# Fused attention and MLP on one core: the copy of a finished half of the context bank moved behind all contexts of its phase

## The chip, the core and the metric

The kernel runs on one NeuronCore of a Trainium2 chip. The engines that matter here are TensorE (PE, with PEld for its weight loads), VectorE (DVE), ScalarE (ACT), GpSimd (POOL) and SyncE (SP); POOL and SP mostly issue DMAs. Each engine works through its own instructions in order, and engines wait for each other through semaphores. The metric is the time of one execution on the device in microseconds (us), taken as a median of runs.

## What is computed

Two branches are computed from the same input `x` (2048 rows of 512, float32), and a gate per row mixes them:

```python
g = sigmoid((x * gate_w).sum(-1, keepdims=True))
# A: attention, 32 query heads of 16, one shared key/value head
q = (x @ wq).reshape(1, 2048, 32, 16).transpose(0, 2, 1, 3)
k, v = x @ wk, x @ wv
p = softmax(einsum("bhqd,bkd->bhqk", q, k) * 16 ** -0.5)
a = einsum("bhqk,bkd->bhqd", p, v).transpose(0, 2, 1, 3).reshape(1, 2048, 512) @ wo
# B: MLP with squared ReLU, 512 -> 1792 -> 512
b = square(maximum(x @ w1 + b1, 0)) @ w2 + b2
out = g * a + (1 - g) * b
```

## The kernel before

**Attention.** The queries are cut into 4 column chunks of 512 positions and 8 groups of 4 heads, so there are 32 *iterations* `it`, and each has two halves `q` of 256 positions. For one half there are 16 key tiles of 128 keys. One *unit* `u` is one key tile of one half for the four heads: a score matmul pair (`score`, line 765) gives 128 keys x 4 heads x 256 positions, ACT takes the exponential into a tile `e` (`exps`, L802), and the *context* of the unit (`context`, L824) multiplies it with the values and adds it up in PSUM. There are 1024 units. Half of a score goes through a PSUM tile `s` of two banks, of which there are two; other scores go through a one-bank tile `x`, from which DVE copies them into `e` first (`score_copy`, L786), and ACT then works on `e` in place. The tile `e` is kept in five buffers of two units each.

**The context bank.** All contexts add up in one PSUM bank, the tile `acc` of 512 columns (`both`). The columns 0 to 255 (`accs[0]`) belong to the half `q = 0` of an iteration and the columns 256 to 511 (`accs[1]`) to `q = 1`. The four heads of a unit go to the four 32-partition quarters of the bank. When the 16th context of a half is done, `finish` copies the 256 columns to an SBUF tile `accs` (on ACT, L882; on DVE, L878 and L930, in the last two iterations). The dependency between the copy and the matmuls is kept for the tile, and not for its columns: a context that is written in program order behind the copy waits until the copy is done, also where it adds to the other half.

**Phases.** PE's instructions are written phase by phase. A `phase` takes some slots of a unit of the projections or the MLP (`M` in the table `PLANS`, L1141; two of them run on two halves of the rows) and puts score matmuls between them (`S0`, `S1`, ... through `s`; `02`, `13` and the like through `x`). Behind it comes `context(range(u, u + m))`, which issues the contexts of `m` units in one go, most often 7 or 6. The scores run ahead of the contexts by `AHEAD` = 4 units, so at the start of a run of contexts ACT still has the exponentials of the phase in its queue, which belong to the contexts of the phases behind. Sixteen is no multiple of 7 or 6, so a half mostly ends inside a run of contexts:

```python
for u in us:
    it, kt, q = place(u)
    ...
    if kt == NK - 1:
        finish(it, q)
```

**Behind the copy.** When both halves of an iteration are copied, SP moves the sums and the denominators to the tiles `oc` and `lq` (L889, L890). Every second iteration `divide` puts four pieces of work on a list for DVE: clamp and test the denominators (`n`, L857 and L858), take the reciprocal (L851), whereupon POOL writes it to DRAM (`ls`, L852) and spreads it with eight DMAs to the tile `lc` (L854), and multiply `oc` with `lc` (L861). Their places among DVE's other work follow from the planner's own clock (`at_pe`, `at_act`, `at_dve`), with fixed allowances: `DIVIDES` = 10 from the copy to the clamp, `SPREADS` = 8 from the reciprocal to the product. The planner's clock holds 0.41 for the copy on ACT and nothing for a wait of the contexts behind it.

Of the kernel before, what the change touches and what calls it, by code (L numbers as in the profile page):

```python
# [14 lines left out]
AF = mybir.ActivationFunctionType  # L15
# [40 lines left out]
HC = CH // 2  # L56
# [109 lines left out]
def mix_kernel(ctx: ExitStack, tc: tile.TileContext, xT, wkv, wq, wo, w12, b1, b2, cst, out):  # L166
    nc = tc.nc
# [63 lines left out]
    with fast, tc.tile_pool(name="at", bufs=1) as at, \  # L231
# [176 lines left out]
        def qnorm(tiles, p8=None):  # L408

            if p8 is None:  # L410
                p8 = aside()
            n = 32 * len(tiles)
            for i, (it, sq) in enumerate(tiles):
                nc.tensor.matmul(p8[32 * i:32 * i + 32], blk, sq, start=True, stop=True, tile_position=(0, 32 * i))
            nrm, tmp = of_tile("nrm"), of_tile("tmp", F32)
            root(nrm[:n], p8[:n], tmp[:n])
            if tiles[0][0] == 0:
                q_direct(RS, nrm, 1, (nc.sync, nc.gpsimd))
            for i, (it, sq) in enumerate(tiles):
                o = qs[it, 0, DH]  # L420
                nc.sync.dma_start(bass.AP(tensor=o.tensor, offset=o.offset,
                                          ap=[[KS * 2 * CH, 4], [CH, 2], [1, CH]]),
                                  nrm[32 * i:32 * i + 8].bitcast(F32))
                done.update((it, it + 1))
# [26 lines left out]
        def act(d, ready=0.0):  # L451

            nonlocal at_act
            at_act = max(at_act, ready) + d
            return at_act

        def dve(d, ready=0.0):

            nonlocal at_dve
            at_dve = max(at_dve, ready) + d  # L460
            return at_dve
# [284 lines left out]
        def place(u):  # L746

            it, k = divmod(u, 2 * NK)
            return (it, k % NK, k // NK) if it else (it, k // 2, k % 2)
# [56 lines left out]
        accs = [None, None]  # L806

        def context(us):

            nonlocal at_pe  # L810
            at_pe += 0.12
            for u in us:
                it, kt, q = place(u)
                at_pe = max(at_pe, made[u] + 0.06) + CONTEXT
                if not both:
                    both.append(ap.tile([128, CH], F32, name="acc"))
                n = 1
                if it == 0:
                    if q == 0:
                        continue  # L820
                    q, n, u = 0, 2, u - 1
                accs[q] = both[0][:, q * HC:q * HC + HC * n]
                for h in range(4):
                    nc.tensor.matmul(accs[q][h * 32:(h + 1) * 32], v_ext[:, kt],  # L824
                                     es[u // 2][:, h % 2 * 2 + h // 2, u % 2 * HC:u % 2 * HC + HC * n],
                                     start=(kt == 0), stop=(kt == NK - 1),
                                     skip_group_check=True, tile_position=(0, h * 32))
                if it == 0:
                    accs[:] = both[0][:, :HC], both[0][:, HC:]
                    if kt == NK - 1:  # L830
                        finish(0, 0)
                    q = 1
                if kt == NK - 1:
                    finish(it, q)
            if narrow:
                at_pe = max(at_pe + 0.2, used_x[0] + 0.05)
                qnorm(narrow.pop(0))
                late.append(True)
                used_x[0] = dve(1.3, at_pe + 0.2) + 0.06
            at_pe += 0.24  # L840
# [21 lines left out]

        sums = []

        def finish(it, q):

            c, gr = divmod(it, NG)
            t, u = divmod(gr, 2)
            if it == NC * NG - 1:
                if q == 0:  # L870
                    side.append(half(accs[0], 0))
                    next(side[-1])
                return
            if q == 0:
                sums.append(at.tile([128, CH], F32, name="accs"))
            a = sums[-1]
            if it == NC * NG - 2:
                nc.vector.tensor_copy(a[:, q * HC:q * HC + HC], accs[q])  # L878
                if q:
                    side.append(turn(a, 0, range(4), LAST_OK))  # L880
                return
            nc.scalar.activation(a[:, q * HC:q * HC + HC], accs[q], AF.Copy)  # L882
            act(0.41, at_pe)
            if q == 0:
                return
            if u == 0:
                ol[c, t] = at.tile([128, CH], F32, name="oc", bufs=2), at.tile([128, LW], F32, name="lq", bufs=2)
            o, l = ol[c, t]
            nc.sync.dma_start(o[u * 64:u * 64 + 64], a[0:128:2])  # L889
            nc.sync.dma_start(l[u * 64:u * 64 + 64], a[1:128:32].rearrange("h (b n) -> h b n", n=LW))  # L890
            if u == 1:
                divisions.extend(divide(o, l, 4 * c + t, at_act + (LANDS if (c, t) == (NC - 1, 2) else DIVIDES)))

                def done():
                    nc.gpsimd.dma_start(oTs[it - 1:it + 1].rearrange("u d n -> (u d) n"), o)
                    complete.add((c, t))

                divisions.append((0.0, 0.0, done))
# [3 lines left out]
        def turn(a, u, js, okc, idle=0):  # L902

            if not o2:
                o2.append(at.tile([128, 4, 2, 4, DH], F32, name="o2", tag="oc", bufs=2))
            js = slice(js[0], js[-1] + 1)
            m = js.stop - js.start
            if m > 2:
                yield
            tp = aside().rearrange("p (j n) -> p j n", j=4)  # L910
            for j in range(m):
                nc.tensor.transpose(tp[:, j], a[:, j * 128:(j + 1) * 128], ident)
            busy(idle)
            p5 = tp[:, :m].rearrange("p j (h d e) -> p j h d e", h=4, e=2)
            l = p5[:, :, :, 0, 1]
            n = at.tile([128, 2, 4, 4], F32, name="nl")[:, :, :m]
            nc.vector.tensor_scalar(n[:, 0], l, L_MIN, L_MAX, op0=OP.max, op1=OP.min)
            nc.vector.scalar_tensor_tensor(n[:, 1], n[:, 0], 1.0, l, op0=OP.mult, op1=OP.is_equal,
                                           accum_out=ok[:, okc:okc + 1])
            nc.vector.reciprocal(n[:, 0], n[:, 0])  # L920
            nc.vector.tensor_tensor(o2[0][:, js, u], p5[:, :, :, :, 0],
                                    n[:, 0].unsqueeze(3).to_broadcast([128, m, 4, DH]), OP.mult)
# [3 lines left out]
        def half(acc, q):  # L926

            js = range(2 * q, 2 * q + 2)
            a = at.tile([128, CH], F32, name="ah", tag="accs" if q else "lc", bufs=1 if q else 2)
            nc.vector.tensor_copy(a[:, :HC], acc)  # L930
            busy(2 * q)
            if not q:
                yield
                yield
            yield from turn(a, 1, js, LAST_OK + 1 + q, 3 * q)
            if q:
                okm = at.tile([128, 1], F32, name="okm")
                nc.vector.tensor_reduce(okm, ok[:, :LAST_OK + 3], AX.X, OP.add)
            else:
                yield  # L940
            r, w = of_tile("or"), of_tile("ol")
            tq = mp.tile([128, CH], F32, name="mm")
            for j in js:
                nc.tensor.transpose(tq[:, j % 2 * 128:j % 2 * 128 + 128],
                                    o2[0][:, j].rearrange("p u h d -> p (u h d)"), ident)
            if q:

                pf = mp.tile([1, 1], F32, name="mm")
                nc.tensor.matmul(pf, okm, cs[:, C_ONE:C_ONE + 1], start=True, stop=True)
                busy(3)  # L950
            nc.scalar.activation(r[:, :HC], tq[:, :HC], AF.Copy)
            if q:
                nc.vector.tensor_scalar(bad, pf, 128.0 * LW * NC * KT - 0.5, None, op0=OP.is_lt)
            nc.vector.tensor_tensor(w[:, :HC], tq[:, :HC], r[:, :HC].bitcast(F32), OP.subtract)
            last[q] = r, w
# [3 lines left out]
        def busy(n):  # L959

            if n and not junk:
                junk.append(sp.tile([128, 2, CH], F32, name="s")[:, 0])
            for _ in range(n):
                nc.tensor.matmul(junk[0], cs[:, :64].bitcast(BF), cs[:, :CH // 2].bitcast(BF), start=True, stop=True)
# [146 lines left out]
        side, units, ended = [], work(), []  # L1111
# [163 lines left out]
        while u < total:  # L1275
# [8 lines left out]
            it = (u + m - 1) // (2 * NK)  # L1284
# [57 lines left out]
```

## Time and profile before

| what | value |
|---|---|
| median of 3 runs | 1387.97 us (1386.97 to 1388.77) |
| profiled execution | 1385.57 us |
| its span, first to last instruction | 1383.8 us |
| PE busy | 1246.4 us (90%) |
| ACT busy | 1060.9 us (77%) |
| DVE busy | 742.4 us (54%) |
| mean granted TensorE clock | 0.957 |
| copies of a half on ACT (L882) | 60, of 385 ns |

The span is the time from the first to the last instruction of the profiled execution; the execution's own time is 1.8 us longer. A share of busy time says how long an engine held an instruction, not how well it was used: the end of a matmul is modelled, and the granted clock tells how fast the array ran. A matmul of the kernel's float32 contexts stands twice in the profile (7 units of 4 heads are 56 rows), since each is run as two passes.

### The profile page before, as it was taken

To read this page: it belongs to the slowest core of one execution; us is meant where nothing else is said; L and a number is where in the kernel's file an instruction comes from. 1 tells how busy PE (TensorE), PEld (TensorE's weight loads), DVE (VectorE), ACT (ScalarE), POOL (GpSimd) and SP (SyncE) were. 2 spreads that over 40 slices of the span, in tenths; PEclk is the share of its full clock that TensorE was granted. 3 is DMA by queue.
4 is the path that set the end of the run, shared out by engine and by line. 5 is a ranking of instruction groups with operands and counts; after the bars stand their busy time and mean duration, and the time that the engine had idled before them with its cause. 6 is when DMAs were issued, how large, how long until landed. Compare 5 with 4: busy or idle time off the path is not lost.

```text
span 1383.8 us, 31763 instructions
## 1 busy us (share of the span) xinstructions
PE 1246.4 (90%) x13686; PEld 801.9 (58%) x13686; DVE 742.4 (54%) x1221; ACT 1060.9 (77%) x1211; POOL 132.4 (10%) x222
## 2 busy tenths in 40 slices
PE   9998889989889899889888988998898889889997
PEld 4565556656556566556555655665565556555663
DVE  6765474656535754537535644646436745547333
ACT  6787686878677887779786877887877868778873
POOL 1002011010010201101012010100102102010100
PEclk9999899999999999999998999999999999999999
DMA  6244321111222212101222212101112212110100
GB/s 218 72 110 108 86 81 43 37 60 52 66 70 70 78 55 86 62 17 50 82 62 79 70 47 86 56 24 48 59 58 78 78 40 94 35 39 30 35 37 33
DMA packets 49338, 89.71 MB, mean 65 GB/s; under 512 B 14362, under 2 KB 14858, under 8 KB 48680
## 3 DMA queue, kind: packets, MB, share of 16 engines
q1 hardware_dynamic: 36664, 64.58, 15.0%
q0 software_dynamic: 12384, 22.77, 5.4%
q8 instruction: 109, 1.79, 0.6%
q14 instruction: 37, 0.30, 0.1%
q10 hardware_dynamic: 144, 0.26, 0.1%
HBM read 61.76 MB, written 21.22 MB: 60 GB/s over the span
## 4 chain that ended last, share of the span: by engine, by line
PE 46%; issue 34%; ACT 11%; POOL 4%; DMA 3%; DVE 2%; DVEq 0%; POOLq 0%; ACTq 0%
PE acc L824 19%; PE mm L1141 14%; PE s L765 9%; ACT e L802 9%; PE x L765 2%; POOL lc L854 2%; DMA ls<-n 1%; DMA lc<-ls 1%; POOL res L697 1%; ACT accs L882 1%; DVE e L786 1%; ACT w2r L500 1%; POOL qs L358 1%; DVE oc L861 0%; ACT w1r L500 0%
## 5 line engine op out<-in xcount | busy, mean ns | idle before, releaser
L802 ACT ACTIVATE e<-s 128x1024 f32<-128x1024 f32 x762 | 749.2, 1027 | 288.1 <-PE s L765 234.6
L786 DVE COPY e<-x 128x512 f32<-128x512 f32 x524 | 362.4, 692 | 573.5 <-PE x L765 461.9
L824 PE MATMUL acc<-e,v_ext 128*32 128x256 f32 (+1 forms) x8064 | 528.3, 410 | 120.9 <-ACT accs L882 119.3
L824 PEld LDWEIGHTS acc<-e,v_ext 128*32 128x32 f32 x8064 | 252.9, 115 | 357.7 <-ACT accs L882 144.3
L765 PE MATMUL s<-qa,k_aug 49*128 49x512 f32 x1524 | 444.8, 418 | 0.1
L765 PEld LDWEIGHTS s<-qa,k_aug 49*128 49x128 f32 x1524 | 235.8, 187 | 98.2 <-ACT e L802 48.6
L802 ACT ACTIVATE e<-e 128x1024 f32<-128x1024 f32 x262 | 277.1, 1058 | 5.8 <-DVE e L786 5.7
L765 PE MATMUL x<-qa,k_aug 49*128 49x512 f32 x524 | 221.7, 423 | 6.3 <-DVE e L786 4.0
L1141 PE MATMUL mm<-w2r,hr 64*128 64x512 f32 x752 | 159.7, 396 | 0.0
L765 PEld LDWEIGHTS x<-qa,k_aug 49*128 49x128 f32 x524 | 97.9, 187 | 35.2 <-DVE e L786 10.6
L1141 PEld LDWEIGHTS mm<-w2r,hr 64*128 64x128 f32 x752 | 108.4, 190 | 13.6 <-issue 0.8
L1141 PE MATMUL mm<-w2l,hr 64*128 64x512 f32 x376 | 92.4, 392 | 0.0
L852 POOL DMA_DIRECT2D ls<-n x15 | 8.5, 564 | 689.4 <-DVE n L851 616.8
L1141 PE MATMUL mm<-xragain,w1r 64*128 64x512 f32 x224 | 67.6, 398 | 0.0
L1141 PE MATMUL mm<-xlagain,w1r 64*128 64x512 f32 x224 | 67.0, 394 | 0.0
L1141 PE MATMUL mm<-xr,w1r 64*128 64x512 f32 x224 | 66.0, 397 | 0.0
L1141 PE MATMUL mm<-xl,w1r 64*128 64x512 f32 x224 | 65.8, 394 | 0.0
L1141 PEld LDWEIGHTS mm<-w2l,hr 64*128 64x128 f32 x376 | 58.4, 186 | 6.6
L854 POOL DMA_DIRECT2D lc<-ls x120 | 58.3, 494 | 30.9 <-DMA ls<-n 30.7
L1141 PE MATMUL mm<-more 64*128 64x512 f32 x216 | 58.5, 394 | 0.0
L1141 PE MATMUL mm<-xragain,w1l 64*128 64x512 f32 x224 | 51.3, 392 | 0.0
L1141 PE MATMUL mm<-xr,w1l 64*128 64x512 f32 x224 | 50.5, 392 | 0.0
(169 smaller groups left out, 1223.3 us busy)
## 6 DMA issues: line engine op xcount, KB each, us to landing
stage<-in_w SPq DMA_DIRECT2D x56, 256.0 KB
qa<-qs SPq DMA_DIRECT2D x186, 64.0 KB
w1f<-in_w SPq DMA_DIRECT2D x28, 256.0 KB
w2f<-in_w SPq DMA_DIRECT2D x28, 256.0 KB
qs<-qr SPq DMA_DIRECT2D x16, 256.0 KB
ress<-res POOLq DMA_DIRECT2D x4, 1024.0 KB, 4.5
qs<-ql POOLq DMA_DIRECT2D x15, 256.0 KB, 7.9
oc<-accs SPq DMA_DIRECT2D x30, 128.0 KB
```

What stands on the lines that cost most here:

```text
L358: eng.dma_start(bass.AP(tensor=o.tensor, offset=o.offset, ap=[[KS * 2 * CH, 4], [CH, 2 * DH], [1, CH]]), src.bitcast(F32))
L500: nc.scalar.activation(out, src, AF.Copy)
L697: nc.gpsimd.tensor_scalar(part, b2t[0], omg[:, s:s + 1], None, op0=OP.mult)
L765: nc.tensor.matmul(dst.rearrange("p (a n) -> p a n", a=2), k_aug[rows, kt * 128:(kt + 1) * 128], qa[it][rows, :, q * HC:q * HC + HC], star ...
L786: nc.vector.tensor_copy(e_half(u)[:, 2 * r:2 * r + 2], x.rearrange("p (a n) -> p a n", a=2))
L802: nc.scalar.activation(e_half(u), src, AF.Exp, scale=SCALE)
L824: nc.tensor.matmul(accs[q][h * 32:(h + 1) * 32], v_ext[:, kt], es[u // 2][:, h % 2 * 2 + h // 2, u % 2 * HC:u % 2 * HC + HC * n], start=(k ...
L852: nc.gpsimd.dma_start(ls[i].rearrange("a (b n) -> (a b) n", b=16), n)
L854: nc.gpsimd.dma_start(wide[16 * k:16 * k + 16], bass.AP(tensor=ls.tensor, offset=ls[i, k].offset, ap=[[0, 16], [1, CH]]))
L882: nc.scalar.activation(a[:, q * HC:q * HC + HC], accs[q], AF.Copy)
L1141: nc.tensor.matmul((self.before if r else self).bank, a[p], b[p], start=not r and i == 0, stop=r == 1 and i == len(self.terms[1]) - 1, ski ...
```

## The change

Inside `context`, a finished half is no longer handed to `finish` at once. The function collects it, with the slice of the bank that it is in, and calls `finish` for all that were collected after the last context of the run has been written. `finish` takes the slice as an argument, because `accs` may have moved on to the next half by then.

```diff
             nonlocal at_pe
             at_pe += 0.12
+            ends = []
             for u in us:
...
                 if it == 0:
                     accs[:] = both[0][:, :HC], both[0][:, HC:]
                     if kt == NK - 1:
-                        finish(0, 0)
+                        ends.append((0, 0, accs[0]))
                     q = 1
                 if kt == NK - 1:
-                    finish(it, q)
+                    ends.append((it, q, accs[q]))
+            for end in ends:
+                finish(*end)
...
-        def finish(it, q):
+        def finish(it, q, acc):
...
-            nc.scalar.activation(a[:, q * HC:q * HC + HC], accs[q], AF.Copy)
+            nc.scalar.activation(a[:, q * HC:q * HC + HC], acc, AF.Copy)
             act(0.41, at_pe)
```

Where a half ends with the last context of a run, nothing moves. The order of the instructions on ACT, POOL and SP is the same as before in the whole program, and so is PE's; on DVE one clamp of denominators (L857), late in the program, stands behind two copies of scores in place of one. What changes is which instruction waits.

The first place is a run of seven contexts on PE, the one that the profile has at 202 us. `s`, `x` and `mm` are PSUM tiles of the scores and of the projections, `acc` is the context bank; a unit is four matmuls here. Before:

```order
L765 MATMUL s<-qa,k_aug 128x512 [waits Activation_49]
L1141 MATMUL mm<-xr_81,w1l 128x512
L765 MATMUL x<-qa,k_aug 128x512 [waits DVE_49]
L765 MATMUL s<-qa,k_aug 128x512
L824 MATMUL acc<-e,v_ext 32x256 x4
L824 MATMUL acc<-e,v_ext 32x256 [waits Activation_49]
L824 MATMUL acc<-e,v_ext 32x256 x23
L765 MATMUL s<-qa,k_aug 128x512 [waits PE_49]
```

The same place with the change:

```order
L765 MATMUL s<-qa,k_aug 128x512 [waits Activation_49]
L1144 MATMUL mm<-xr_81,w1l 128x512
L765 MATMUL x<-qa,k_aug 128x512 [waits DVE_49]
L765 MATMUL s<-qa,k_aug 128x512
L825 MATMUL acc<-e,v_ext 32x256 x28
L765 MATMUL s<-qa,k_aug 128x512 [waits Activation_49]
```

The second unit's first matmul had to wait for ACT, and 24 matmuls stood behind it; now the 28 matmuls have no wait among them. The first score of the next phase now names ACT itself; it needs the exponential that frees its tile `s`, which the wait inside the contexts had covered before.

The second place is ACT's queue at the same time: two exponentials, the rounding of a weight tile (`more`), the copy, and the first exponential of the next phase. Before:

```order
L802 ACTIVATE e<-e 128x4x256 [waits DVE_49]
L802 ACTIVATE e<-s 128x4x256
L500 ACTIVATE more<-stage 128x512
L882 ACTIVATE accs<-acc 128x256
L802 ACTIVATE e<-s 128x4x256 [waits PE_49,Activation_49]
```

With the change:

```order
L802 ACTIVATE e<-e 128x4x256 [waits DVE_49]
L802 ACTIVATE e<-s 128x4x256
L500 ACTIVATE more<-stage 128x512
L885 ACTIVATE accs<-acc 128x256 [waits PE_49]
L802 ACTIVATE e<-s 128x4x256 [waits PE_49,Activation_49]
```

The copy keeps its place in ACT's queue and now waits for PE there, for the contexts of the run that are written ahead of it.

More of the change, by code (lines that the diff above doesn't have):

```diff
@@ L870, in finish @@
                 if q == 0:
-                    side.append(half(accs[0], 0))
+                    side.append(half(acc, 0))
                     next(side[-1])
@@ L877, in finish @@
             if it == NC * NG - 2:
-                nc.vector.tensor_copy(a[:, q * HC:q * HC + HC], accs[q])
+                nc.vector.tensor_copy(a[:, q * HC:q * HC + HC], acc)
                 if q:
```

## The prediction

> **What bounds the kernel now.** The page's first part, busy time by engine, says that PE is nearest to its limit:
>
> ```profile
> PE 1246.4 (90%) x13686; PEld 801.9 (58%) x13686; DVE 742.4 (54%) x1221; ACT 1060.9 (77%) x1211; POOL 132.4 (10%) x222
> ```
>
> The waits by engine then say what stops PE, and what the others wait for (columns: total us, times, longest):
>
> ```profile
> PEld acc L824 <- ACT accs L882: 144.3, 52, 7.0
> PE acc L824 <- ACT accs L882: 119.3, 52, 6.6
> ...
> ACT e L802 <- PE s L765: 234.6, 134, 6.5
> ...
> PEld s L765 <- ACT e L802: 48.6, 123, 0.8
> ...
> DVE oc L861 <- DMA lc<-ls: 13.1, 9, 4.1
> ```
>
> One wait stands out: 52 of the 60 copies stop the context matmuls. The PE row counts from the modelled end of the last matmul and the PEld row from the last weight load, so the true stop lies between 119.3 and 144.3 us. ACT and DVE mostly wait for PE; neither is the pacer over the whole kernel.
>
> To see what one such stop is, I cut the stretch around 200 us at the phases' starts: a phase without a copy, the next phase's scores, the stop, the contexts left, and the phase after (columns: us, busy us of PE, PEld, DVE, ACT and POOL with counts, granted clock, DMA):
>
> ```profile
> 189.76:197.54 7.78, 7.78 (x99) 5.30 (x96) 6.81 (x12) 7.78 (x10) 0.00 (x0) 1.00 0.34 103
> 197.54:202.17 4.63, 4.63 (x43) 3.55 (x39) 2.85 (x5) 4.05 (x5) 0.00 (x0) 1.00 0.32 93
> 202.17:206.66 4.49, 0.64 (x10) 0.15 (x9) 3.16 (x5) 3.67 (x5) 0.00 (x0) 1.00 0.18 52
> 206.66:211.07 4.41, 4.41 (x48) 2.03 (x48) 0.00 (x0) 0.00 (x0) 0.00 (x0) 0.61 0.09 32
> ```
>
> The timelines of PE and of ACT show the cause:
>
> ```profile
> 202.17 0.64 PE L824 MATMUL acc<-e,v_ext 128*32 128x256 f32 x8
> 206.66 4.48 PE L824 MATMUL acc<-e,v_ext 128*32 128x256 f32 x48 [3.85 <-ACT accs L882]
> ```
>
> ```profile
> 204.80 1.01 ACT L802 ACTIVATE e<-s 128x1024 f32<-128x1024 f32 x1
> 205.71 0.63 ACT L500 ACTIVATE more<-stage 128x512 fp32r<-128x512 f32 x1
> 206.22 0.38 ACT L882 ACTIVATE accs<-acc 128x256 f32<-128x256 f32 x1
> 211.91 2.89 ACT L802 ACTIVATE e<-s 128x1024 f32<-128x1024 f32 x3 [5.30 <-PE s L765]
> ```
>
> The first context of the run closes a half. Its copy takes 0.38 us, but stands on ACT behind exponentials that are only needed by a later phase; PE idles 3.85 us for it with 48 matmuls queued. Two things follow. ACT, done at 206.6, idles 5.30 us, because the next scores come late: the time is lost to both. And the 48 matmuls run at a clock of 0.61 and take 4.41 us. Scores and contexts together took 13.53 us (197.54 to 211.07), where the phase ahead took 7.78 for as much work: 5.75 us lost by one copy.
>
> **What the change removes.** (a) *The stop.* The run of contexts has no wait in it any more. In the example 5.75 us are lost; 3.85 are the PE row's wait, and the clock costs (1 - 0.61) x 4.41 = 1.72, so 0.18 is missing from the PE row. With 0.2 on each of 52 waits, the stop is worth 119.3 + 10.4 = 130 us (bounds 119.3 and 144.3).
>
> (b) *The slow clock behind it.* The row of cores gives the clock over the span:
>
> ```profile
> core 0: 1383.8 us, clock 0.957
> ```
>
> That is (1 - 0.957) x 1383.8 = 59.5 us of lost full-clock time. Some of it passed while PE was idle anyway, as behind the longest stop (two windows, then windows behind two other stops, with those stops' rows of the timeline):
>
> ```profile
> 136.00:138.00 2.00, 0.00 (x0) 0.00 (x0) 1.42 (x3) 0.10 (x1) 0.83 (x2) 0.50 0.27 17
> 138.00:140.00 2.00, 0.00 (x0) 0.00 (x0) 1.76 (x3) 2.00 (x3) 0.16 (x1) 0.50 0.15 43
> ```
>
> ```profile
> 290.56:292.86 2.30, 2.30 (x40) 1.20 (x41) 0.00 (x0) 0.00 (x0) 0.00 (x0) 1.00 0.18 61
> ...
> 371.50:374.50 3.00, 3.00 (x24) 1.49 (x18) 0.00 (x0) 0.13 (x1) 0.00 (x0) 0.50 0.18 52
> ```
>
> ```profile
> 290.56 2.37 PE L824 MATMUL acc<-e,v_ext 128*32 128x256 f32 x40 [2.61 <-ACT accs L882]
> ```
>
> ```profile
> 371.03 2.58 PE L824 MATMUL acc<-e,v_ext 128*32 128x256 f32 x24 [2.08 <-ACT accs L882]
> ```
>
> Four idle us at 0.50 are 2 of the 59.5; with a few shorter ones and the span's ends I take 52 as paid by matmuls (bounds 40 and 59.5). [...]
>
> A check on (a) and (b) together: the contexts behind the first iteration are 7936 rows, 8 to a unit, so 992 units. A clean phase of seven takes 7.79 us; the first such phase starts at 70.35 and the last context ends at 1369.24.
>
> ```profile
> L824 PE MATMUL acc<-e,v_ext 128*32 128x256 f32 x7936 | 513.3, 407 | 120.9 <-ACT accs L882 119.3 <-DVE accs L878 1.1 <-DVE ah L930 0.5
> ```
>
> ```profile
> 646.05:653.84 7.79, 7.79 (x98) 5.23 (x94) 5.84 (x10) 6.39 (x8) 0.00 (x0) 1.00 0.11 34
> ```
>
> ```profile
> 70.35 0.49 PE L765 MATMUL s<-qa,k_aug 49*128 49x512 f32 x1
> ```
>
> ```profile
> 1368.60 0.64 PE L824 MATMUL acc<-e,v_ext 128*32 128x256 f32 x8
> ```
>
> 992 x 7.79 / 7 = 1104 us at the clean rate, 1298.9 in fact: 195 us are lost to everything. (a) and (b) claim 182 of them; the other 13 stay.
>
> **What it adds.** (c) *The copy waits for the rest of the run, and the next phase's exponentials queue behind it on ACT.* Eight copies already stand behind all contexts, because a half ended with its run. Two such phases, and the phase behind the second:
>
> ```profile
> 265.99:273.93 7.94, 7.94 (x98) 5.14 (x95) 5.80 (x10) 7.94 (x11) 0.00 (x0) 1.00 0.10 35
> 872.04:880.00 7.96, 7.96 (x99) 5.16 (x95) 5.85 (x10) 7.96 (x11) 0.00 (x0) 1.00 0.30 96
> 880.00:887.79 7.79, 7.79 (x100) 5.55 (x96) 6.47 (x14) 6.55 (x8) 2.52 (x5) 1.00 0.15 52
> ```
>
> They take 0.15 and 0.17 us more than 7.79; ACT is busy throughout, and in the next phase it has slack again (6.55 of 7.79). So 52 copies at 0.16 cost 8 us. Below, a copy could cost nothing where ACT has slack; above, its whole 0.38, which is 20 us. SP's move of the sums and POOL's spreading follow the copy as before; both only wait longer for it, in program terms by what was left of the run, and the loads queued behind SP's move go to tiles that DVE frees later.
>
> (d) *DVE's wait for the spread denominators.* From the reciprocal (L851) to the product (L861), the DMAs out and back take some 8.7 us, whatever PE does. Two cases on DVE, the first with no stop of PE between, the second with one, and that stop:
>
> ```profile
> 632.40 0.35 DVE L851 RECIPROCAL n<-n 128x32 f32<-128x32 f32 x1
> ...
> 641.11 0.69 DVE L861 TENSOR_TENSOR oc<-oc,lc 128x512 f32<-128x512 f32 x1 [1.28 <-DMA lc<-ls]
> ```
>
> ```profile
> 303.64 0.35 DVE L851 RECIPROCAL n<-n 128x32 f32<-128x32 f32 x1
> ...
> 313.07 0.69 DVE L861 TENSOR_TENSOR oc<-oc,lc 128x512 f32<-128x512 f32 x1 [0.59 <-DMA lc<-ls]
> ```
>
> ```profile
> 308.44 1.50 PE L824 MATMUL acc<-e,v_ext 128*32 128x256 f32 x24 [1.20 <-ACT accs L882]
> ```
>
> Behind the waiting product stand DVE's copies of `x`, which PE waits for: the first case's phase took 8.84 (below), 1.05 over the clean 7.79.
>
> ```profile
> 637.21:646.05 8.84, 8.24 (x98) 5.27 (x94) 6.43 (x11) 8.22 (x11) 2.55 (x6) 1.00 0.27 83
> ```
>
> In the second case 1.20 us of stop hid as much of the chain; without it DVE waits about 1.8. With 15 products, a wait of about 1.2 each is 18 us; the 13.1 of now are partly open already and some 5 to 8 of the 18 stay hidden, so I add 10 us (bounds 0, and 22 if every stop between a reciprocal and its product, 1.5 us on average, turns into a wait).
>
> **The sum.** The profiled execution is 1385.57, 2.4 under the median. 1385.6 - 130 - 52 + 8 + 10 = 1221.6, and with the 2.4 it is 1224 us. What is late next is mixed: PE at its clean rate, with ACT close behind (1060.9 busy of 1224 is 87%).
>
> **Rivals.**
> *The spread chain takes over.* Every product waits 2 to 3 us with PE idle behind it, as in the 4.1 of the longest, and some of these halve the clock again: 15 x 2.5 = 38 in place of 10, and 15 x 0.5 x 1.7 = 13 for the clock: 1224 + 41 = 1265. For it: the chain's length doesn't shrink with the phases. Against: where no stop lies between, the wait was 1.28. Chance 0.09.
> *The wait moves to the next phase's first score.* It names ACT in the new order. If it must see ACT's queue emptied, it waits for the last exponential and the copy, about 1.01 + 0.38 behind the run's end in half of the phases: 52 x 0.7 = 36, so 1260. Against: it needs a `s` tile freed two exponentials earlier, and the two phases of (c) show no such wait. Chance 0.04.
> *The clock doesn't come back.* If only the longest stops halve the clock, the eight of 3.85 us and more (seven of 3.85 in the timeline, and the longest, 6.6) answer for 8 x 1.7 = 14 of the 52, and the rest has another cause and stays: 1224 + 38 = 1262. Against: the half clock behind the stop of 2.08. Chance 0.04. [...]
> *Slower.* If ACT were the pacer, the stop would be where it catches up, and taking it away would only move it, while each copy now holds ACT idle for the contexts left, 24 of 56 matmuls or 1.4 us on average: 1388 + 52 x 1.4 = 1461. This decides once ACT has no idle time ahead of a phase's first exponential; it has 234.6 us, with 5.30 right behind a copy. Chance 0.02.
> *The change doesn't do what it says*: the new rows of PE show the wait gone; chance 0.01 for no difference.
>
> **The numbers.** The forecast has 0.80. Its own bounds run from 1200, where the check's 195 come back but for the 8 of (c), to 1246, with the least of (a) and the most of (d). Above it the first three rivals end at 1260 to 1265. A range of 1205 to 1252 holds the forecast's case with a margin for the 6 us between its upper bound and the next case, and leaves out the 0.20 of the others. A measurement of this kernel can tell about 0.2% from no change; faster by more than that has 0.97, within it 0.01, slower 0.02.
>
> **What would show it.** Right: no wait of `acc` for `accs` on PE in mid-run; clock 0.99 or more; phases with a copy at about 7.95; ACT behind a copy idle under 1 us; DVE's wait for `lc` at 15 to 30 us in total. Wrong: PE waits of many us before `s` or `x`, a clock still near 0.96, or a DVE wait for `lc` above 40.

## The result, and the profile after

| | before | after |
|---|---|---|
| median of 4 runs | 1388.37 us (1386.97 to 1389.23) | 1229.62 us (1226.17 to 1236.39) |
| profiled execution | 1385.57 us | 1226.17 us |
| granted clock in it | 0.957 | 0.994 |

The ratio is 0.8863, with a 95% interval of 0.8825 to 0.8902: the changed kernel takes 11.4% less time. The forecast was 1224, in the terms of the profiled execution 1221.6 against 1226.17.

Line numbers behind the change are three higher: the context is L825 now, the copy L885, the product of the sums L864. First the busy times of the page and the row of cores:

```profile
PE 1194.5 (98%) x13686; PEld 788.2 (64%) x13686; DVE 743.2 (61%) x1221; ACT 1058.2 (86%) x1211; POOL 131.4 (11%) x222
```

```profile
core 0: 1224.4 us, clock 0.994
```

PE is busy for 98% of a shorter span. ACT and DVE do the same work as before and only lose their waiting. The waits by engine say which (columns: total us, times, longest):

```profile
ACT e L802 <- PE s L765: 61.6, 97, 3.2
...
DVE oc L864 <- DMA lc<-ls: 25.9, 13, 6.5
...
PE x L765 <- DVE e L786: 17.2, 14, 3.7
...
ACT accs L885 <- PE acc L825: 2.6, 6, 0.5
```

The two rows of contexts that waited for a copy, 119.3 and 144.3 us, are gone altogether. The copy waits for PE instead, 2.6 us in 6 waits. ACT's wait for scores went from 234.6 us to 61.6: that was the same idle time seen from the other side. What grew is DVE's wait for the spread denominators, from 13.1 to 25.9, and behind it PE's wait for `x`.

The same seven contexts that stopped at 202 us are at 190.07 us now (timeline of PE):

```profile
190.07 3.23 PE L825 MATMUL acc<-e,v_ext 128*32 128x256 f32 x56
```

One row of 56 takes 3.23 us, where 0.64, a stop of 3.85 and 4.48 at a clock of 0.61 stood. ACT at that place, and at a second copy 72 us later:

```profile
192.71 1.01 ACT L802 ACTIVATE e<-s 128x1024 f32<-128x1024 f32 x1
193.61 0.63 ACT L500 ACTIVATE more<-stage 128x512 fp32r<-128x512 f32 x1
194.13 0.38 ACT L885 ACTIVATE accs<-acc 128x256 f32<-128x256 f32 x1
194.39 2.87 ACT L802 ACTIVATE e<-s 128x1024 f32<-128x1024 f32 x3
```

```profile
265.75 0.38 ACT L885 ACTIVATE accs<-acc 128x256 f32<-128x256 f32 x1
266.39 1.03 ACT L802 ACTIVATE e<-s 128x1024 f32<-128x1024 f32 x1 [0.26 <-PE s L765]
```

No 5.30 us of idle time stands behind the copy any more. Cut into phases as before (columns: us, busy us of PE, PEld, DVE, ACT and POOL with counts, granted clock, DMA), with the copies of 194.13 and 265.75 in the second and the third, and a late phase with a copy:

```profile
185.43:193.23 7.80, 7.80 (x98) 5.41 (x95) 5.82 (x10) 6.41 (x8) 0.00 (x0) 1.00 0.30 85
193.23:201.19 7.96, 7.96 (x98) 5.16 (x94) 6.19 (x11) 7.96 (x11) 0.00 (x0) 1.00 0.17 53
...
265.61:273.40 7.79, 7.79 (x99) 5.35 (x95) 4.62 (x7) 6.75 (x9) 0.00 (x0) 1.00 0.29 87
...
1099.73:1107.66 7.93, 7.93 (x99) 5.17 (x95) 6.78 (x12) 7.93 (x11) 0.00 (x0) 1.00 0.23 68
```

The copy costs 0.17 where ACT is busy throughout (7.96 of 7.96, and 0.14 in the late phase) and nothing where ACT has slack (6.75 of 7.79). Behind the first iteration, twelve phases of seven units are over 0.6 us longer than 7.79. In eleven of them DVE waits for the spread denominators; the twelfth, at 944.70, is taken up in the last section. Six of the eleven:

```profile
132.01:147.01 15.00, 10.79 (x100) 7.01 (x96) 7.75 (x12) 9.02 (x10) 3.04 (x6) 0.77 0.38 98
...
208.98:218.06 9.08, 8.09 (x99) 5.29 (x96) 4.03 (x6) 7.51 (x9) 4.57 (x7) 1.00 0.19 54
423.73:433.99 10.26, 8.55 (x100) 5.29 (x96) 6.37 (x10) 7.97 (x10) 8.74 (x11) 1.00 0.21 49
567.62:580.12 12.50, 9.77 (x98) 5.67 (x94) 6.64 (x11) 8.48 (x11) 4.06 (x9) 0.86 0.21 64
```

```profile
1083.17:1091.95 8.78, 8.19 (x98) 5.08 (x94) 6.22 (x10) 8.21 (x11) 2.48 (x5) 1.00 0.26 85
1010.25:1020.59 10.34, 8.03 (x99) 5.28 (x95) 4.63 (x7) 6.75 (x9) 4.01 (x8) 1.00 0.43 134
```

Four of them are 7.21, 2.47, 4.71 and 2.55 over 7.79; the seven others are 0.7 to 1.3 over (the first at 208.98, the last at 1083.17), 6.8 together. That makes some 24 us. The wait at 1010.25, 2.77 us, is not in the 25.9: the profile puts it down to another DMA, which POOL issued right behind the eight. The two longest phases also lost the clock (0.77 and 0.86). This is DVE in the first of them, from the reciprocal to the product:

```profile
120.33 0.35 DVE L854 RECIPROCAL n<-n 128x32 f32<-128x32 f32 x1
...
134.84 0.69 DVE L864 TENSOR_TENSOR oc<-oc,lc 128x512 f32<-128x512 f32 x1 [6.54 <-DMA lc<-ls]
```

And POOL, which issues the DMAs in between:

```profile
119.05 0.70 POOL L358 DMA_DIRECT2D qs<-ql  x1 [8.03 <-DVE w2l L495]
121.00 0.59 POOL L855 DMA_DIRECT2D ls<-n  x1 [1.25 <-DVE n L854]
129.15 3.87 POOL L857 DMA_DIRECT2D lc<-ls  x8 [7.57 <-DMA ls<-n]
```

The chain took 14.5 us here, not 8.7: POOL idled 7.57 us until the write of the reciprocals, issued 2 us behind a transfer of queries, had landed, and then eight issues of 0.48 each passed before the last piece was on its way. At the second longest phase the chain took 10.9 us (562.76 to 573.61); there POOL idled 3.06 us until the write had landed. PE waited behind DVE's product; its rows there and at the second of the two phases:

```profile
136.19 0.79 PE L765 MATMUL x<-qa,k_aug 49*128 49x512 f32 x1 [3.68 <-DVE e L786]
...
574.95 0.79 PE L765 MATMUL x<-qa,k_aug 49*128 49x512 f32 x1 [2.73 <-DVE e L786]
```

### The profile page after: what moved, and what is told of

It is laid out like the page before. It is cut to its first block, busy times and chain, and to the rows that moved or that the text cites. A ratio compares the mean times of both kernels' runs of the same rounds, so it can differ in the third digit from the quotient of the medians.

```text
span 1224.4 us, 31785 instructions
## 1 busy us (share of the span) xinstructions
PE 1194.5 (98%) x13686; PEld 788.2 (64%) x13686; DVE 743.2 (61%) x1221; ACT 1058.2 (86%) x1211; POOL 131.4 (11%) x222
## 4 chain that ended last, share of the span: by engine, by line
PE 43%; issue 42%; POOL 5%; DMA 5%; DVE 3%; ACT 1%; DVEq 0%; POOLq 0%; SPq 0%; ACTq 0%
PE acc L825 17%; PE mm L1144 14%; PE s L765 9%; POOL lc L857 3%; DMA ls<-n 3%; PE x L765 2%; DMA lc<-ls 1%; DVE e L786 1%; POOL res L697 1%; DMA xf<-in_xT 0%; POOL out L221 0%; PE mm L299 0%; DVE oc L864 0%; ACT e L802 0%; PE mm L203 0%
## 5 line engine op out<-in xcount | busy, mean ns | idle before, releaser
L802 ACT ACTIVATE e<-s 128x1024 f32<-128x1024 f32 x762 | 748.5, 1029 | 120.7 <-PE s L765 61.6
L825 PE MATMUL acc<-e,v_ext 128*32 128x256 f32 (+1 forms) x8064 | 475.8, 385 | 0.0
L825 PEld LDWEIGHTS acc<-e,v_ext 128*32 128x32 f32 x8064 | 246.4, 110 | 198.6 <-issue 54.7
L765 PEld LDWEIGHTS s<-qa,k_aug 49*128 49x128 f32 x1524 | 230.7, 185 | 97.0 <-ACT e L802 73.4
L1144 PEld LDWEIGHTS mm<-w2r,hr 64*128 64x128 f32 x752 | 105.5, 187 | 12.8 <-issue 0.8
L857 POOL DMA_DIRECT2D lc<-ls x120 | 58.2, 492 | 32.8 <-DMA ls<-n 32.5
```

The costliest lines, as they stand in the source:

```text
L765: nc.tensor.matmul(dst.rearrange("p (a n) -> p a n", a=2), k_aug[rows, kt * 128:(kt + 1) * 128], qa[it][rows, :, q * HC:q * HC + HC], star ...
L802: nc.scalar.activation(e_half(u), src, AF.Exp, scale=SCALE)
L857: nc.gpsimd.dma_start(wide[16 * k:16 * k + 16], bass.AP(tensor=ls.tensor, offset=ls[i, k].offset, ap=[[0, 16], [1, CH]]))
L1144: nc.tensor.matmul((self.before if r else self).bank, a[p], b[p], start=not r and i == 0, stop=r == 1 and i == len(self.terms[1]) - 1, ski ...
```

## The experiments

The theory to test has three parts. The copy stopped PE for as long as ACT's queue ahead of it was. PE's idling there is what halved the clock. What remains over the clean rate in the changed kernel is DVE's wait for the spread denominators. The rivals: that the gain is the clock's alone, or that the clock has another cause; that ACT paces the kernel, so that a stop taken away comes back elsewhere; that the copies behind the runs, and not the denominators, cost what remains. Every time is a median beside the kernel before on the same chip.

**The changed kernel again**, on the chip of three of the runs below (half the dose, two more us, one DMA):

> The changed kernel once more, beside the next three on the same chip. Theory: 1229.6 us as before, within 0.6%; the clock between 0.985 and 0.994, since waits of DVE for the spread denominators (lc) halve the clock behind some of them and not always the same ones. Rival (the spread between its runs, 1226 to 1236, comes from the chip): then the next three kernels spread as much.

Measured: 1224.72 us (1222.45 to 1227.33), ratio 0.8838 [0.8809, 0.8868], clock 0.995, DVE's wait for `lc` 27.0 us in 14. The result and its picture repeat, and these three runs are compared with 1224.72.

**Half the dose.** The copies of `q = 0` go behind the run, those of `q = 1` stay between contexts:

```diff
                 if kt == NK - 1:
-                    ends.append((it, q, accs[q]))
+                    if q == 0:
+                        ends.append((it, q, accs[q]))
+                    else:
+                        for end in ends:
+                            finish(*end)
+                        ends.clear()
+                        finish(it, q, accs[q])
```

> The changed kernel with half of the change undone: the copy of the half q = 0 goes behind the run of contexts, that of q = 1 is issued between two contexts as before. Theory: each copy in mid-run costs for itself. In the profile of before the stops of the copies of q = 1 are 56 of the 119 us, and 13 of the 30 stretches at half clock stand behind them, so 56 x 1.09 + 13 x 1.7 = 83 us come back: 1305 to 1315, PE's wait of acc for accs at 50 to 62 us, clock 0.97 to 0.98. Rival (ACT is the pacer, and a stop taken away here makes the next one longer): the remaining stops grow, PE's wait above 75 us, time above 1330.

Measured: 1298.14 us (1296.26 to 1300.07), ratio 0.9368 [0.9339, 0.9398], clock 0.982. Its wait:

```profile
PE acc L825 <- ACT accs L891: 55.6, 25, 3.9
```

25 of 52 stops are left, with 47% of the wait (55.6 of 119.3), and 73 of the 163 us (45%) are still lost. The price is paid per copy, about 3 us each with its clock. Were ACT the pacer, half of the stops taken away would have brought little or nothing.

**The copy two contexts later**, still between contexts where more of the run is left:

```diff
             for u in us:
+                if ends and u - ends[0][3] > 2:
+                    finish(*ends.pop(0)[:3])
                 it, kt, q = place(u)
```

> The changed kernel with the copy issued two contexts after the end of its half where the run has more than two left, and behind the run otherwise. Theory: ACT's queue in front of the copy stays, so a stop is shorter by two contexts, 0.9 us, and gone where two or fewer are left; of the profile of before 35 stops stay, 95 us less 35 x 0.9 = 64 us on PE's row, 70 in truth, and only the 12 to 14 that are still over 2 us halve the clock, 22 us: 1228 + 70 + 22 = 1310 to 1325, PE's wait 55 to 70 us, clock 0.975 to 0.985. Rival (each copy that has contexts behind it costs the same): 35 of 52 stops stay whole, 95 us on PE's row, time 1345 or more.

Measured: 1308.42 us (1300.86 to 1310.29), ratio 0.9431 [0.9412, 0.945], clock 0.984.

```profile
PE acc L827 <- ACT accs L887: 69.9, 35, 8.5
```

```profile
197.01 1.50 PE L827 MATMUL acc<-e,v_ext 128*32 128x256 f32 x24
201.51 1.93 PE L827 MATMUL acc<-e,v_ext 128*32 128x256 f32 x32 [2.99 <-ACT accs L887]
```

The number of stops is the expected one, 35, PE's wait is at the top of its range, and the time is 1.6 us under its range. The 35 must be compared with the same 35 of before, those with three or more units left behind the copy: in the trace of before they are 96.8 us of the 119.3, 2.8 each, and here they are 2.0 each. So nearly all of the two contexts' time (0.9 us) came off each stop. In the example (the two rows) the stop is 2.99 in place of 3.85, with two more units ahead of it: the copy runs when ACT's queue lets it, and PE waits for what is left by then. Of the 49.4 us of wait that went, 22.5 are the 17 stops that are gone, where nothing of the run stands behind the copy any more, and 27 come from the stops that stay. Only the longest grew, from 6.6 to 8.5: ACT, ahead of that copy, waited 5.95 us for DVE (3.12 before).

**The copy on DVE**, between contexts as before the change:

```diff
-            nc.scalar.activation(a[:, q * HC:q * HC + HC], accs[q], AF.Copy)
-            act(0.41, at_pe)
+            nc.vector.tensor_copy(a[:, q * HC:q * HC + HC], accs[q])
+            dve(0.42, at_pe)
```

> The kernel before, with the copy on DVE in place of ACT, still between two contexts. Theory: the stop is the length of the queue that stands ahead of the copy. On DVE that is at most the eviction of a unit of the MLP, 3.2 us from the start of a run and less as contexts pass, so 52 stops of 0.5 to 1.5 us and few stretches at half clock: PE's wait of acc for accs 35 to 75 us, clock above 0.98, time 1275 to 1325. Rival (a copy in mid-run costs the same wherever it runs): PE's wait near 119 us, time near 1388.

Measured: 1304.68 us (1301.78 to 1312.47), ratio 0.9434 [0.939, 0.9478], clock 0.988.

```profile
PE acc L824 <- DVE accs L882: 74.0, 52, 7.5
```

```profile
135.74 0.69 DVE L861 TENSOR_TENSOR oc<-oc,lc 128x512 f32<-128x512 f32 x1 [5.04 <-DMA lc<-ls]
```

```profile
139.34 4.24 PE L824 MATMUL acc<-e,v_ext 128*32 128x256 f32 x48 [7.45 <-DVE accs L882]
```

All 52 stops are there, with 74 us in place of 119 by PE's rows (longest 7.5 in place of 6.6). The stop stays whichever engine copies, and its length changes with the engine, though the work copied is the same: it goes by what that engine has ahead of the copy. In 22 of the 52 the stop is 0.55 us, little more than the copy itself (0.42). At the longest (the two rows above), DVE waited 5.04 us for the spread denominators, and the product and four more instructions went before the copy at 138.87.

**PE kept busy during the stop, first try.** Before a copy in mid-run, PE multiplies zeros into the finished half (nothing is added to the sums, no work is left out), for about the length of the stop; the moving operand is the `e` of the last unit:

```diff
                 if kt == NK - 1:
+                    for _ in range((0, 1, 1, 3, 3, 5, 5)[us[-1] - u] if 0 < it < NC * NG - 2 else 0):
+                        for h in range(4):
+                            nc.tensor.matmul(accs[q][h * 32:(h + 1) * 32], zero,
+                                             es[u // 2][:, h % 2 * 2 + h // 2, u % 2 * HC:u % 2 * HC + HC],
+                                             start=False, stop=True,
+                                             skip_group_check=True, tile_position=(0, h * 32))
                     finish(it, q)
```

> The kernel before, with matmuls of an all-zero stationary tile added to the half that has just ended, ahead of its copy (5 units' worth of 0.45 us where 5 or 6 contexts are left in the run, 3 where 3 or 4 are, 1 where 1 or 2 are). They add zeros to the sums, and PE is busy in a part of each stop instead of idle; the copy waits no longer than for ACT's queue. Theory: the stops stay as long as they were (130 us of no progress), but the half clock behind them goes, so clock 0.985 or more and 1388 - 40 to 50 = 1338 to 1348 us; the contexts behind a stop run at full clock. Rival (the half clock is not caused by PE's idling): clock 0.957 still, time 1388 or more. Rival (the stops are cheap and the clock is the whole gain): below 1300.

Measured: 1398.07 us (1394.65 to 1398.80), ratio 1.0091 [1.0056, 1.0125], clock 0.979. The expectation missed, because the added matmuls made the stops longer:

```profile
PE acc L826 <- ACT accs L890: 86.4, 52, 4.5
...
ACT e L804 <- PE acc L838: 41.6, 18, 3.0
```

The added matmuls (L838) read `e` longer, and ACT waited 41.6 us for the buffer, ahead of the very copy that PE waits for. From the start of the last context ahead of a stop to the start of the first behind it, all 52 stops come to 174.3 us, where they were 139.0; with the contexts held up so much longer, the time doesn't settle what the clock costs.

**The same with a moving operand that nobody writes**, the constant tile:

```diff
-                                             es[u // 2][:, h % 2 * 2 + h // 2, u % 2 * HC:u % 2 * HC + HC],
-                                             start=False, stop=True,
+                                             cs[:, :HC], start=False, stop=True,
```

> The kernel before with all-zero matmuls in the stops once more, as in the run with zeros before, but their moving operand is a constant tile and no longer the tile e of the last unit: there, ACT's next exponentials had to wait for the added matmuls to leave e (41.6 us of waits), which lengthened the queue that the copy stands in, so the stops of 3.85 us were not filled at all and the run told nothing. Now the added matmuls (71 us in all) lie inside the stops. Theory: PE's wait of acc for accs falls by some 60 us to about 60, because the zeros take its place, and no progress is made for as long as before; the clock rises to 0.985 or more, and the time is 1388 - 40 to 50 = 1338 to 1350. Rival (the half clock does not come from PE's idling): clock 0.957, 1385 or more. Rival (the clock is the whole gain): 1260 or less.

Measured: 1342.88 us (1340.42 to 1346.71), ratio 0.9675 [0.9649, 0.9701], clock 0.995. Its wait, and the group of the added matmuls (their count, busy us and mean ns):

```profile
PE acc L826 <- ACT accs L889: 54.4, 52, 4.1
```

```profile
L838 PE MATMUL acc<-cs,zero 128*32 128x256 f32 x1264 | 77.7, 379 | 0.0
```

And PE at the stop of the example:

```profile
199.61 0.64 PE L826 MATMUL acc<-e,v_ext 128*32 128x256 f32 x8
200.07 2.34 PE L838 MATMUL acc<-cs,zero 128*32 128x256 f32 x40
204.10 2.80 PE L826 MATMUL acc<-e,v_ext 128*32 128x256 f32 x48 [1.70 <-ACT accs L889]
```

The stop is about as long as before (2.34 busy and 1.70 idle, for 3.85 idle), but the 48 matmuls behind it take 2.80 us in place of 4.48. From context to context, all 52 stops come to 142.3 us, against 139.0 before. With the contexts held up as long as ever, the clock alone brings 1388.2 - 1342.9 = 45 us (42 to 49 by the interval of the ratio). So PE's idling is what took the clock, and the clock is a quarter to a third of the gain; the rest, 1342.9 down to 1229.6, is the stop less what the change adds.

**Each copy made twice**, in the changed kernel:

```diff
-            nc.scalar.activation(a[:, q * HC:q * HC + HC], acc, AF.Copy)
+            for _ in range(2):
+                nc.scalar.activation(a[:, q * HC:q * HC + HC], acc, AF.Copy)
```

> The changed kernel with each copy made twice on ACT, behind its run of contexts. The cost of a copy there was put at 0.16 us in the prediction (8 us in all), and at most 0.38 (20 us); the phases of the changed kernel show less, some 0.15 us in one phase of three and nothing in the others, 4 us in all. Theory by the trace: 60 more copies cost 3 to 8 us against the changed kernel, 1228 to 1236. Rival (ACT at 86% is about to be the bound): 15 us or more, 1240 and above.

Measured: 1238.75 us (1235.02 to 1242.14), ratio 0.8937 [0.8899, 0.8975], clock 0.993. That is 9 us over 1229.62 and 14 over 1224.72, 0.15 to 0.23 for each of 60 more copies on average, above what was expected. A wait that the changed kernel did not show has come up; the second row is the phase of the copy that stood at 194.13 there:

```profile
PE s L765 <- ACT e L802: 6.2, 20, 0.5
```

```profile
195.58:203.94 8.36, 8.06 (x99) 5.18 (x95) 6.19 (x11) 8.33 (x12) 0.00 (x0) 1.00 0.16 50
```

The phase took 7.96 with one copy and takes 8.36 with two: where the first used up ACT's slack, the second is paid in full, and where ACT had slack it is free (the phase of 265.61 is 7.79 in both). Even so, doubling all of them costs less than a tenth of what the stops had cost.

**Two more us between reciprocal and product.** The changed kernel with the planner's allowance at 10:

```diff
-LANDS, DIVIDES, WRITES, SPREADS, SURE = 6.0, 10.0, 14.0, 8.0, 0.7
+LANDS, DIVIDES, WRITES, SPREADS, SURE = 6.0, 10.0, 14.0, 10.0, 0.7
```

> The changed kernel with the planner's allowance SPREADS at 10 in place of 8, which puts 12 of the 15 products of the division one to four score copies further back in DVE's queue. Theory: of the 35 us that the changed kernel's phases take over their clean lengths, some 24 stand in the phases where DVE waits for lc (25.9 us in total), so the wait falls under 8 us, the clock rises to 0.996 or more, and the time to 1207 to 1216. Rival (DVE is simply full in these phases, and a later product only moves the delay): the wait falls but PE's waits for x stay, 1226 to 1233.

Measured: 1212.62 us (1211.25 to 1214.92), ratio 0.8754 [0.8728, 0.878], DVE's wait for `lc` 9.8 us in 3, a little over the 8 that were expected, the longest still 6.8 (the first division). The clock, 0.995, is no higher than in the changed kernel.

**One DMA in place of eight** for the spreading, at the old allowance:

```diff
-                for k in range(8):
-                    nc.gpsimd.dma_start(wide[16 * k:16 * k + 16], bass.AP(tensor=ls.tensor, offset=ls[i, k].offset,
-                                                                          ap=[[0, 16], [1, CH]]))
+                nc.gpsimd.dma_start(wide, bass.AP(tensor=ls.tensor, offset=ls[i, 0].offset,
+                                                  ap=[[CH, 8], [0, 16], [1, CH]]))
```

> The changed kernel with one DMA in place of eight that spread the denominators, at SPREADS 8. Theory: the eight issues on POOL take 3.9 us of the chain of 8.7 us between reciprocal and product; with one of some 1 us the chain is 5.5 to 6.5 us and the wait for lc falls from 25.9 to under 8 us, time 1207 to 1216. Rival (one large DMA lands as much later as it is issued earlier): wait and time as in the changed kernel, 1226 to 1233.

Measured: 1210.61 us (1209.89 to 1216.67), ratio 0.8748 [0.8715, 0.8782]. The wait has all but gone, save at the first division, where POOL still waited 6.65 us for the reciprocals to land (its row, then DVE's waits):

```profile
127.75 0.64 POOL L856 DMA_DIRECT2D lc<-ls  x1 [6.65 <-DMA ls<-n]
```

```profile
DVE oc L863 <- DMA lc<-ls: 5.7, 2, 5.4
```

Two quite different edits of the chain alone, a longer allowance and fewer issues, return 12 and 14 us of the changed kernel's time.

**Both, for the first division too**: one DMA, and an allowance of 20 for the first product only:

```diff
-                    (0.72, ready + SPREADS, lambda: nc.vector.tensor_tensor(o, o, wide, OP.mult)))
+                    (0.72, ready + (SPREADS if i else 20.0), lambda: nc.vector.tensor_tensor(o, o, wide, OP.mult)))
```

> The changed kernel with one DMA in place of eight for the spread, and the product of the very first division five score copies later, because its denominators stand behind another DMA of POOL's queue for 7 us. With one DMA alone the changed kernel came to 1210.6 us, with 5.4 us of DVE's wait and the half clock behind it left at the first product. Theory: these go too, which is worth the 6.8 us that the phase is too long in that kernel: 1202 to 1207, clock 0.998 or more. Rival (the first product's wait hides something else that is late there, the queries' tiles): 1209 to 1213.

Measured: **1204.11 us** (1203.00 to 1206.69), ratio 0.8695 [0.8664, 0.8727], clock 0.999. This is the fastest kernel of the study and beats both.

```profile
PE x L765 <- DVE e L786: 2.3, 3, 1.5
...
DVE oc L863 <- DMA lc<-ls: 0.2, 1, 0.2
```

The wait for `lc` is 0.2 us, and the time is 20.6 us under the changed kernel's 1224.72 and 25.5 under its 1229.62.

**The same with the allowance of 10 for all other products:**

> The fastest kernel so far (one DMA for the spread, the first product late) with SPREADS at 10 on top, so that the other products stand one to four score copies further back as well. Theory: DVE's wait for lc is 0.2 us there already, so nothing is left to gain: 1202 to 1207. Rival (a later product frees DVE's queue where POOL's own work slows DVE): 1200 or less.

Measured: 1204.41 us (1203.77 to 1206.60), ratio 0.8682 [0.8667, 0.8698], clock 0.998. With no wait left in the chain, more room in it brings nothing.

## Why the prediction was right, and where it was off

**The stop (a) and the clock (b)**, 182 us together, were right in kind and close in size. All 52 waits went and none came back elsewhere. The profiled time fell by 159.4; with what the change added (3 us for the copies, and for the denominators 12.8, by which DVE's wait grew, or 24, the loss of all eleven phases), (a) and (b) returned 175 to 186. For the clock alone 52 us were forecast; the core rows say (59.5 - (1 - 0.994) x 1224.4) = 52, but some of that passed while PE idled, and the filled stops give the part that matmuls paid and got back: 45, inside the bounds of 40 and 59.5. The filled run still loses (1 - 0.995) x 1342.5 = 6.7, and 45 and 6.7 are the 52; the changed kernel, which still loses 7.3 behind other waits, got back about as much as the filled one.

**The copies behind the runs (c)** were put at 0.16 each. The size per copy was right where ACT is busy throughout: 0.17 at 193.23, 0.14 at 1099.73, and 0.14 to 0.25 in 14 phases between them, 3 us in all. In nearly all others ACT had slack and the copy was free, so the term was 3, not 8. The doubled copies show that this was the slack's doing: without it a copy costs 0.40, its whole length.

**The denominators (d)** are the step that was mis-sized. The prediction had a wait of about 1.2 for each product, 18 us in all, of which 10 new. The wait was 25.9 in all, and the phases that it lengthens lost some 24 us; taking it away returned 20 to 25 in the fastest kernel. Two things were missed. "The DMAs out and back take some 8.7 us, whatever PE does" is not so for the first division, where the write was issued 2 us behind a transfer of queries and the chain took 14.5, nor at the second longest phase, with 10.9. The trace of before had this to read: its first division took 12.1 (124.46 to 136.58), and its wait is the longest there, the 4.1. And twice the clock fell behind PE's idling there (3.68 and 2.73 us), 15.00 x 0.23 + 12.50 x 0.14 = 5 us. This was the first rival's mechanism, in two phases of fifteen.

By the prediction's own check: from the first phase to the end of the last context (below) are 1138.6 us, so 34.6 are lost over the clean 1104, where the forecast left 13 + 18 = 31.

```profile
70.51 0.49 PE L765 MATMUL s<-qa,k_aug 49*128 49x512 f32 x1
...
1208.49 0.64 PE L825 MATMUL acc<-e,v_ext 128*32 128x256 f32 x8
```

The forecast's 31 were 18 for the denominators (8 of them inside the 13), 8 for the copies and 5 for all else. Measured are some 24, 3 and 8; of the 8, 2.0 are in the phase at 944.70 (last section), and the rest is spread over phases of little excess and the kernel's end. So (d) was 6 too small, (c) 5 too large and the remainder 3 too small; the profiled time came out 4.6 above the forecast. That it came so close is in part luck, since these errors go both ways. The median stands 3.5 over the profiled execution, where 2.4 was taken.

**The rivals.** The clock did come back (0.994). The third rival, that only the longest stops halve it, does not fit: in the trace of before the clock was 0.50 behind a stop of 2.08 us and 1.00 behind one of 2.61, and in the changed kernel it fell in the phase with the gap of 2.73 too (0.86 over the phase), not only in the one with 3.68 (0.77). So the length of the gap alone does not decide; what does was not shown. The wait at the next phase's first score did not come: PE's row for it comes up only when each copy is made twice, with 6.2 us. ACT is no pacer, as the half dose shows. That rival's price had a slip: 24 of 56 matmuls is the mean over all 60 copies, and over the 52 it is 28, so 1388 + 52 x 1.6 = 1471.

**What stays open.** The dependency itself was not tried: no run copied one half while the contexts of the other added up in the same bank. Why the changed kernel's runs spread by 10 us (by 5 on the second chip) was not tested; they go with the clock (0.994 at 1226.17, 0.985 at 1236.39), and the fastest kernel, with no such waits, spreads by 3.7 at 0.998 to 0.999.

## What to carry to other kernels

A short instruction that a busy engine needs before it can go on costs that engine the queue that is left ahead of it on the other engine, here 3.85 us for a copy of 0.38: look at who stands ahead of the 0.38 us, and put the instruction where nothing of the waiting run is behind it. Idle time of PE is paid twice where the clock falls with it (45 us here, beside stops of 119.3), so price a stop with the matmuls behind it. When stops of the pacing engine go, look for chains that they had hidden (DVE's wait for `lc` went from 13.1 to 25.9 us), and time the slowest instance of such a chain, here 14.5 us, not a typical one, here 8.7.

## What the runs showed of the hardware that was not expected

DVE ran slower, a cast 2.12 us in place of 0.43, beside an elementwise instruction on POOL. In the changed kernel POOL multiplies four tiles around 941 us:

```profile
941.38 6.35 POOL L697 TENSOR_SCALAR res<-big,omg 128x512 f32<-128x512 f32 x4
```

DVE's same two instructions 10 us before and during it:

```profile
934.71 0.43 DVE L195 CAST hr<-big 128x512 fp32r<-128x512 f32 x1
935.17 0.69 DVE L196 TENSOR_TENSOR hr<-big,hr 128x512 fp32r<-128x512 f32 x1
...
944.19 2.12 DVE L195 CAST hr<-big 128x512 fp32r<-128x512 f32 x1
946.34 1.05 DVE L196 TENSOR_TENSOR hr<-big,hr 128x512 fp32r<-128x512 f32 x1
```

The cast is longer by 1.69 us, about one of the four POOL instructions (6.35 / 4 = 1.59); PE then waited 1.69 for a score copy, and the phase from 944.70 took 9.75 (PE busy for 8.06):

```profile
944.70:954.45 9.75, 8.06 (x99) 5.31 (x95) 8.20 (x11) 7.93 (x10) 4.12 (x4) 1.00 0.41 124
```

It is no single case: in the traces of before, of the changed kernel and of the doubled copies, 45 of the 47 casts `hr<-big` of each take 0.43 us, and the two of each that took longer (0.80 and 2.12, 0.58 and 2.12, 0.58 and 2.12) ran while POOL was at this multiplication. No run here took the POOL work away, so the cause is not shown.

The same small transfer, the reciprocals' write, landed at very different times: POOL idled 7.57 us for it in the first division, where a transfer of queries had gone out 2 us ahead, and 1.44 in this one, where POOL had issued nothing for 20 us:

```profile
931.76 0.54 POOL L855 DMA_DIRECT2D ls<-n  x1 [20.39 <-DVE n L854]
933.74 3.87 POOL L857 DMA_DIRECT2D lc<-ls  x8 [1.44 <-DMA ls<-n]
```

That the queries are the reason is likely: in the traces of before, of the changed kernel, of the doubled copies and of the one DMA, the first division's write was issued 4.0, 2.0, 1.8 and 2.5 us behind their transfer, POOL idled 4.52, 7.57, 8.17 and 6.65 us for it, and could go on 9.1, 10.1, 10.6 and 9.7 us after it had issued the queries. No run took that transfer away. Nor would it be the only thing that holds up the write: at 563.65 POOL had issued nothing for 62 us, and the wait was 3.06.
